# Scores by row groups only: the padded copies of Q leave a mixed attention and convolution kernel

## The chip, the cores and the metric

One core of one Trainium2 chip. The metric is the device time of one execution in microseconds; the kernel before is given as the median of three runs. The engines are named PE (matrix products), PEld (its weight loads), DVE, ACT, POOL and SP; SP, ACT and POOL also issue DMAs. "Granted clock" is the share of full speed that the throttle left the matrix engine.

## The reference

Two blocks read sequences of 2048 positions and 448 channels and are mixed by a gate per position. Block A is attention with 16 heads of 28 channels that share one key and one value head. Block B is a convolution over time, per channel, whose kernel K comes from 256 complex modes.

```python
g = sigmoid((x * gate_w).sum(-1))
# A
q = x @ wq ; k = x @ wk ; v = x @ wv              # q: 16 heads of 28; k, v: one head
p = softmax(q . k * 28 ** -0.5) ; a = concat(p @ v) @ wo
# B
K[d, l] = Re(sum_n C[d,n] * exp(dt[d] * A[d,n] * l) * dt[d] * B[d,n])     # l = 0 .. 2047
b = causal_conv(u, K) + u * Dskip
out = g * a + (1 - g) * b
```

## The kernel before

**Attention.** A score tile is one head of one group of four heads against 128 keys and 512 queries. There are 16 rounds (four query blocks by four head groups) of 64 tiles, 1024 tiles in all, taken in sets of three and two by turns; 410 sets. For each set PE writes the tiles into PSUM banks (`qk`), ACT takes the exponential of the whole set in one instruction (L1153), and two sets later PE multiplies four exponentials at a time with the values, each into 32 of 128 columns of the array (`pv`, L1163). Five PSUM banks hold scores, one holds the sums of a round, two are lent to everything else. ACT has nothing to do in the long run but these exponentials.

A score product has only 29 rows (28 channels and one for a bound of the maximum). The kernel has two forms. The row form (L1125) puts each head on its own 32 rows of the array, so that the tiles of one set run at the same time. The full form (L1133) uses all 128 rows with a copy of Q, `qM`, in which the rows of the other heads are zero; its tiles run one after the other. The first six sets are of row form, the next eight of full form, and from then on sets of three are of row form and sets of two of full form. `qproj` makes Q of a round on PE and DVE, and then four DMAs on POOL's queue copy it into `qM`, which POOL set to zero at the start.

**Convolution.** For each of 14 groups of 32 channels DVE builds tables of powers (`masters`, `tables`), PE multiplies them to K (`kgen`, L915) in two halves, each with its own PSUM bank and its own two evacuations by DVE (L926, L930), and POOL's queue writes K to memory. SP's queue then loads it back as Toeplitz blocks (`tload`, four channels each, 112 blocks) into one of four buffers in `T`, or, later on, into the used part of `U`. `conv` multiplies a block with `U`, the transposed input; four channels run at once, each on 32 columns of the array (L974). DVE scales, PE transposes back (L995), DVE adds to the output tile `O` (L1003).

**Order.** The order of each engine's instructions is fixed ahead by a list scheduler in `Prog.schedule`. It has a price for every operation, a constant for POOL's use of DVE's memory port (`PORT`), a slack for late consumers (`SLACK`), and a priority per operation; scores come first, convolution fills what is left. Engines take their instructions strictly in that order.

**End.** `norm` divides a round's sums by their last column. For the first 15 rounds the denominators go through memory on POOL's queue. For the last one PE gathers them (L1048), DVE takes 16 reciprocals per partition (L1052) and spreads them (L1054), PE transposes them back (L1059), and DVE multiplies 512 columns (L1063). `tail` makes the last projections (L1077) and adds them to `O` (L1021). All output goes out on SP's queue: the columns of the last two channel groups in one transfer of 64-byte pieces (`outz`), everything else ahead of it.

## Time and profile before

| | |
|---|---|
| median of 3 runs | 523.14 us (521.81 to 524.54) |
| the profiled execution, its own time | 521.35 us |
| its span, first to last instruction | 519.4 us |
| first exponential starts, last one ends | 27.7 us, 504.2 us |
| ACT, busy time of all / of the exponentials | 483.6 us / 465.8 us |
| PE, PEld, DVE, POOL, busy time | 431.1, 192.9, 447.5, 161.6 us |
| granted clock, mean of 27.7 to 112 us / of 112 to 504.2 us | 0.74 / 1.00 |
| DMA engines, mean busy share of the same two stretches | 0.71 / 0.94 |

An engine's busy time says how long it had an instruction in work; the busy time of PE includes the pipeline's latency, so PE can show as busy without being at its peak. What counts is which engine the others wait for: time in which ACT has no exponential is lost for good, and so is what lies ahead of the first exponential and behind the last.

### The profile page before, as it was taken

How to read it: one execution, taken by the hardware profiler on the slowest of the kernel's cores; microseconds unless marked ns; L12 is line 12 of the kernel's file. 1: busy time of each engine (PE TensorE's matmuls, PEld its weight loads, DVE VectorE, ACT ScalarE, POOL GpSimd, SP SyncE). 2: the span in 40 equal slices, each digit the busy share in tenths (PEclk: the TensorE clock that was granted, in tenths of full speed). 3: DMA queues.
4: the chain of work that ended last, by engine and by line, in shares of the span. 5: the costliest groups of instructions: out<-in, count | busy, mean ns of one | idle time of the engine just before them, and what ended most of it. 6: DMA issues, size and time to landing. Idle time of an engine off the chain costs nothing.

```text
span 519.4 us, 18307 instructions
## 1 busy us (share of the span) xinstructions
PE 431.1 (83%) x8123; PEld 192.9 (37%) x8234; DVE 447.5 (86%) x798; ACT 483.6 (93%) x431; POOL 161.6 (31%) x299
## 2 busy tenths in 40 slices
PE   5778967888878789988878889988888889798884
PEld 4522111324334334434333434433344344443342
DVE  3877899999999999999999979999999989952123
ACT  3699899999999999999999999999999999899980
POOL 5014321612413442424214242432414233315100
PEclk9858587979999999999999999999999999999998
DMA  8995395497991998899998899899996999999996
GB/s 263 259 236 157 28 79 139 120 364 251 288 365 54 321 350 256 271 342 347 316 367 296 279 373 276 285 336 350 329 330 212 304 370 353 346 282 305 376 365 172
DMA packets 121997, 144.31 MB, mean 278 GB/s; under 512 B 53860, under 2 KB 60564, under 8 KB 121920
## 3 DMA queue, kind: packets, MB, share of 16 engines
q1 hardware_dynamic: 112368, 133.06, 81.3%
q0 software_dynamic: 8896, 9.53, 6.8%
q8 instruction: 64, 1.05, 0.8%
q10 hardware_dynamic: 656, 0.57, 0.4%
q14 instruction: 13, 0.11, 0.1%
HBM read 128.76 MB, written 5.23 MB: 258 GB/s over the span
## 4 chain that ended last, share of the span: by engine, by line
ACT 40%; DVE 36%; PE 17%; DMA 3%; issue 2%; ACTq 0%; SPq 0%
ACT expT L1153 40%; DVE tab L868 6%; PE psS L1133 4%; DVE tab L880 3%; DVE tab L879 3%; DVE tab L878 3%; PE psB L1163 3%; PE psS L1125 3%; DVE tab L890 3%; DVE tab L877 3%; DMA T<-KP_scratch 2%; DVE tmp L886 2%; DVE msq L811 1%; DVE cst L984 1%; PE psX L915 1%
## 5 line engine op out<-in xcount | busy, mean ns | idle before, releaser
L1153 ACT ACTIVATE expT<-psS 128x1536 bf16<-128x1536 f32 (+1 forms) x410 | 465.8, 1349 | 8.1 <-PE psS L1125 5.3
L1133 PE MATMUL psS<-qM,kT 128*128 128x512 bf16 x308 | 106.6, 402 | 35.5 <-ACT expT L1153 21.7
L1125 PE MATMUL psS<-qT,kT 29*128 29x512 bf16 x609 | 84.0, 401 | 27.8 <-ACT expT L1153 23.4
L1163 PE MATMUL psB<-expT,vaug 128*32 128x512 bf16 x1024 | 105.4, 403 | 1.1 <-ACT expT L1153 0.6
L137 POOL DMA_DIRECT2D KP_scratch<-kstg x112 | 62.3, 563 | 121.3 <-DVE kstg L930 114.6
L868 DVE TENSOR_TENSOR tab<-tab,mbf 128x512 bf16<-128x512 bf16 (+3 forms) x56 | 64.5, 1152 | 0.0
L1163 PEld LDWEIGHTS psB<-expT,vaug 128*32 128x32 bf16 x1024 | 26.2, 93 | 83.2 <-issue 78.7
L137 POOL DMA_DIRECT2D qM<-qT x64 | 32.0, 507 | 67.9 <-DVE qT L786 42.9
L1125 PEld LDWEIGHTS psS<-qT,kT 29*128 29x128 bf16 x609 | 20.1, 91 | 72.6 <-ACT expT L1153 60.2
L1133 PEld LDWEIGHTS psS<-qM,kT 128*128 128x128 bf16 x415 | 26.0, 98 | 54.8 <-ACT expT L1153 40.2
L137 POOL DMA_DIRECT2D rdenB<-R_scratch x60 | 30.5, 514 | 38.5 <-DMA R_scratch<-denT 27.9
L880 DVE TENSOR_TENSOR tab<-tab 128x128 bf16<-128x128 bf16 (+4 forms) x70 | 41.8, 597 | 0.0
L879 DVE TENSOR_TENSOR tab<-tab 128x128 bf16<-128x128 bf16 (+4 forms) x70 | 41.8, 597 | 0.0
L974 PE MATMUL psS<-T,U 128*32 128x128 bf16 (+7 forms) x1600 | 39.0, 220 | 2.2 <-DMA T<-KP_scratch 1.3
L974 PEld LDWEIGHTS psS<-T,U 128*32 128x32 bf16 (+7 forms) x1600 | 27.1, 94 | 18.1 <-issue 12.2
L137 POOL DMA_DIRECT2D denT<-acc x15 | 10.9, 726 | 69.1 <-DVE acc L1030 45.0
L890 DVE TENSOR_TENSOR tab<-tab,tmp 128x4096 bf16<-128x4096 bf16 x14 | 32.1, 2290 | 0.1
L878 DVE TENSOR_TENSOR tab<-tab,mbf 128x4096 bf16<-128x4096 bf16 x14 | 31.9, 2280 | 0.1
L877 DVE TENSOR_TENSOR tab<-tab,mbf 128x4096 bf16<-128x4096 bf16 x14 | 32.0, 2283 | 0.0
L974 PE MATMUL psX<-T,U 128*32 128x128 bf16 (+7 forms) x1216 | 29.9, 223 | 1.0 <-issue 0.9
L974 PEld LDWEIGHTS psX<-T,U 128*32 128x32 bf16 (+7 forms) x1216 | 21.0, 95 | 14.7 <-issue 11.3
L915 PE MATMUL psX<-tab 128*32 128x64 bf16 x1024 | 24.8, 241 | 1.1 <-DVE qT L786 0.4
(153 smaller groups left out, 517.1 us busy)
## 6 DMA issues: line engine op xcount, KB each, us to landing
T<-KP_scratch SPq DMA_DIRECT2D x176, 512.0 KB, 8.7
U<-KP_scratch SPq DMA_DIRECT2D x48, 512.0 KB, 9.6
rdenB<-R_scratch POOLq DMA_DIRECT2D x60, 64.0 KB, 5.7
U<-cst SPq DMA_DIRECT2D x1, 3584.0 KB, 18.7
qM<-qT POOLq DMA_DIRECT2D x64, 32.0 KB, 5.1
tab<-in_A_x_dram SPq DMA_DIRECT2D x4, 448.0 KB, 6.2
O<-in_A_x_dram SPq DMA_DIRECT2D x16, 112.0 KB, 2.7
O<-cst SPq DMA_DIRECT2D x1, 1792.0 KB, 28.6
```

The lines of the kernel that those rows point to most:

```text
L137: return [e.dma_start(o, i, **kw) for o, i in pairs]
L868: vo(lambda e, dst=dst, src=src, mri=mri: e.tensor_tensor(dst, src, mri, ALU.mult), 4 * n, done + mk(lv), [kr, ki, tk])
L877: vo(lambda e, src=src, mi=mi, tv=tv: e.tensor_tensor(tv, src, mi, ALU.mult), 2 * n, done + mk(lv), [tk])
L878: vo(lambda e, dst=dst, src=src, mr=mr: e.tensor_tensor(dst, src, mr, ALU.mult), 2 * n, done + mk(lv), [kr, ki, ("gap", s)])
L879: vo(lambda e, dc=dc, tc=tc: e.tensor_tensor(dc[0], dc[0], tc[1], ALU.subtract), n, [tk, kr], [kr])
L880: vo(lambda e, dc=dc, tc=tc: e.tensor_tensor(dc[1], dc[1], tc[0], ALU.add), n, [tk, ki], [ki])
L890: vo(lambda e: e.tensor_tensor(tab.v(0, P, FM, [[4, 1024], [1, 4]]), tab.v(0, P, lo + 124, [[CG, 32], [-4, 32], [1, 4]]), rho.v(0, P, 0, [ ...
L974: r = e.matmul(ps.v(32 * j, 32 - 2 * n, 128 * k, [[1, 128]]), self.U.v(0, P, (4 * gi + j) * 32 + 2 * n, [[1, 32 - 2 * n]]), tbuf.v(0, P, t ...
L1125: r = e.matmul(self.psS.v(0, P, 512 * b, [[1, 512]]), kT.v(32 * h, DH + 1, 128 * kt, [[1, 128]]), qT.v(32 * h, DH + 1, 512 * (i % 2), [[1, ...
L1133: return e.matmul(self.psS.v(0, P, 512 * b, [[1, 512]]), kT.v(0, P, 128 * kt, [[1, 128]]), self.qM.v(0, P, (i % 2) * XQ + 512 * h, [[1, 51 ...
L1153: pg.op("act", lambda e: e.activation(expT.v(0, P, 512 * es[0], spread(es, n)), self.psS.v(0, P, 512 * bs[0], spread(bs, n)), AF.Exp, scal ...
L1163: r = e.matmul(self.psB.v(32 * h, 32, 0, [[1, 512]]), vaug.v(0, P, 32 * kt, [[1, 32]]), expT.v(0, P, 512 * ring[t], [[1, 512]]), start=(kt ...
```

## The change

All score sets take the row form. `qM`, its zeroing and its 64 DMAs go. The memory that they held becomes a fifth Toeplitz buffer. The rest comes with it:

- `kgen` writes both halves into one PSUM bank, and DVE evacuates them with two instructions instead of four; the eight DMAs follow together.
- `U` holds channels in pairs: POOL's eight copies move 4-byte units, the zero fill and the duplicating DMA have half as many pieces, and `conv` reads every second element. The filling of `U` is taken behind the preparation of the parameters, whose scratch moves from `mbf` to `O`.
- `masters` of the first block of channels writes its squares to the two buffers by turns.
- The last `norm` multiplies the sums with a matrix that puts each head's denominator on all of its 32 rows, in two halves of 256 columns; DVE takes reciprocals of all 256 columns and multiplies.
- The last four output tiles go out whole, two on ACT's queue and two on SP's, and `outz` covers only the first twelve.
- In the loads of the start, the weights of K and V come first and `log_dt` before `wq`.
- The scheduler's constants for POOL's port and for DVE's slack change, and one for DMA time. The order of all engines is planned anew with these.

```diff
-NTR = 4
+NTR = 5
...
-    PORT = 750.0
+    PORT = 0.7
...
-    SLACK = {"pe": 500.0, "dve": 1000.0}
+    SLACK = {"pe": 500.0, "dve": 500.0}
...
-                if e == "pool" and o.ns >= 900.0:
-                    free["dve"] = max(free["dve"], r) + self.PORT
+                if e == "pool" and o.ns >= 500.0:
+                    free["dve"] = max(free["dve"], r) + self.PORT * o.ns
...
-        self.qM = sb("qM", 2 * 4 * 512, BF)
...
-        for k in range(2):
-            pm(V(self.qM, k * XQ, XQ), 0.0, 1800, [("qM", k)], 1.5)
...
-            pg.dma([(self.qM.v(32 * h, 32, s * XQ + 512 * h, [[1, 512]]), self.qT.v(32 * h, 32, 512 * s, [[1, 512]]))
-                    for h in range(4)], (128, 1024), f"qm{s}", rd=[("q", s)], wr=[("qM", s)], pr=0, eng="pool", extra=4500)
...
-            if s < 6 or s >= 14 and len(ts) == 3:
-                rd = set()
-                ...
-                pg.op("pe", row, 220, rd=sorted(rd, key=str), wr=bk, pr=0, mode="q", ni=2 * len(ts))
-            else:
-                for t, b in zip(ts, bs):
-                    i, kt, h = dec(t)
-                    pg.op("pe", lambda e, t=t, b=b: full(e, t, b), 220, rd=[("qM", i % 2), ("kT", kt // 4)],
-                          wr=[("b", b)], pr=0, mode="f", ni=2)
+            pg.op("pe", row, 220, rd=sorted(rd, key=str), wr=bk, pr=0, mode="q", ni=2 * len(ts))
...
-                pg.op("pool", lambda e, k=k, j=j: e.tensor_copy(
-                    self.U.v(0, P, 8 * k + j, [[32, D], [1, 2]]),
-                    self.O.v(0, P, (8 * k + j) * D, [[1, D], [D, 2]])), 1080,
+                pg.op("pool", lambda e, k=k, j=j: e.tensor_copy(
+                    U2.v(0, P, 8 * k + j, [[32, D // 2], [1, 2]]),
+                    O2.v(0, P, (8 * k + j) * D // 2, [[1, D // 2], [D // 2, 2]])), 560,
...
-                                     self.U.v(0, P, (4 * gi + j) * 32 + 2 * n, [[1, 32 - 2 * n]]),
+                                     self.U.v(0, P, (2 * gi + j // 2) * 64 + 4 * n + j % 2, [[2, 32 - 2 * n]]),
...
+        pg.op("dve", lambda e: e.tensor_copy(ko.v(0, P, 0, [[64, 8], [1, 63]]), G.v(0, P, 0, [[64, 8], [1, 63]])),
+              el(504), rd=[X], wr=["kst"], pr=2, unlock=G)
...
+        for hf, b in enumerate((1, 6)):
+            ...
+            pg.op("pe", lambda e, bc=bc, hv=hv: e.matmul(bc, self.identf.v(0, P, 0, [[1, P]]), hv, start=True, stop=True,
+                                                         tile_position=(0, 0), skip_group_check=True),
+                  440, rd=[("acc", i % 2), "msq"], wr=[("b", b)], pr=0)
+            pg.op("dve", lambda e, bc=bc, rv=rv: e.reciprocal(rv, bc), el(256), rd=[("b", b)] + ["rd"] * hf, wr=[("rd", hf)] + ["rd"] * (1 - hf), pr=0)
+            pg.op("dve", lambda e, on=on, hv=hv, rv=rv: e.tensor_tensor(on, hv, rv, ALU.mult), el(256),
+                  rd=[("acc", i % 2), ("rd", hf)], wr=[("on", g + hf)], pr=0)
...
-            pg.dma([(dram(self.out, tl * P * D, [[D, P], [1, D0]]), self.O.v(0, P, D * tl, [[1, D0]]))],
-                   (128, 832), f"out{tl}", rd=[("O", 3)], pr=1)
...
+        pg.dma([(dram(self.out, D0, [[D, P], [P * D, 12], [1, 32]]), self.O.v(0, P, D0, [[D, 12], [1, 32]]))],
+               (1024, 64), "outz", rd=[("Oz", q) for q in range(3)], pr=1)
+            pg.dma([(dram(self.out, tl * P * D, [[D, P], [1, D]]), self.O.v(0, P, D * tl, [[1, D]]))],
+                   (128, 896), f"out{tl}", rd=[("O", 3 + tt), ("Oz", 3 + tt)], pr=1, eng=("act", "sp")[tt % 2])
```

## The prediction

> **What bounds the kernel now.** First the page, parts 1 and 5, then busy time by stretch.

> ```profile
> PE 431.1 (83%) x8123; PEld 192.9 (37%) x8234; DVE 447.5 (86%) x798; ACT 483.6 (93%) x431; POOL 161.6 (31%) x299
> ...
> L1153 ACT ACTIVATE expT<-psS 128x1536 bf16<-128x1536 f32 (+1 forms) x410 | 465.8, 1349 | 8.1 <-PE psS L1125 5.3
> L1133 PE MATMUL psS<-qM,kT 128*128 128x512 bf16 x308 | 106.6, 402 | 35.5 <-ACT expT L1153 21.7
> L1125 PE MATMUL psS<-qT,kT 29*128 29x512 bf16 x609 | 84.0, 401 | 27.8 <-ACT expT L1153 23.4
> ```

> ACT is the bound. From the first exponential (27.7) to the end of the last (504.2) pass 476.5 us, 465.8 of them exponentials and only 8.1 waiting, nearly always for PE's scores. The change leaves all 410 exponentials as they are. So it can gain at most those 8.1, something ahead of 27.7 and something of the 15.2 us behind 504.2; it can lose whatever makes PE late.

> Next, PE and the granted clock (columns: PE, PEld, DVE, ACT, POOL busy, clock, DMA share, GB/s):

> ```profile
> 50.60:54.00 3.40, 3.24 (x15) 0.59 (x15) 3.30 (x5) 3.40 (x3) 3.21 (x4) 0.50 0.00 0
> 54.00:57.40 3.40, 3.36 (x20) 0.56 (x16) 3.29 (x5) 3.35 (x4) 2.91 (x3) 0.50 0.00 0
> ...
> 60.80:64.20 3.40, 3.18 (x12) 0.62 (x12) 1.89 (x8) 1.55 (x3) 0.00 (x0) 0.50 0.77 59
> ...
> 101.80:105.20 3.40, 2.06 (x20) 0.52 (x20) 3.40 (x8) 3.40 (x4) 1.34 (x3) 1.00 0.89 298
> 105.20:108.60 3.40, 2.73 (x14) 0.48 (x12) 3.40 (x4) 3.40 (x4) 0.56 (x1) 0.50 1.06 399
> 108.60:112.00 3.40, 3.40 (x43) 1.16 (x43) 3.40 (x6) 2.47 (x3) 0.00 (x0) 0.50 1.06 392
> ...
> 27.70:112.00 84.30, 68.17 (x527) 19.72 (x536) 75.87 (x142) 80.04 (x71) 26.17 (x41) 0.74 0.71 150
> 112.00:504.20 392.20, 338.21 (x7266) 154.90 (x7366) 348.14 (x611) 388.75 (x344) 127.78 (x236) 1.00 0.94 310
> ```

> The clock is 1.00 or 0.50 and changes in steps of 3.41 us. Up to 112 us it is half in five stretches, although PE shows as 95% busy in some of them; from 112 on, when convolution fills PE, it never falls. At half clock ACT starves: 4.3 us are idle before 112, only 3.5 in the 392 us after.

> Last the exponentials' pace, the price of a reciprocal, and the end (start, duration, engine, line):

> ```profile
> 45.94 6.89 ACT expT L1153 x6
> ...
> 52.88 1.04 PE psS L1133 x2
> 53.92 0.55 PE psB L1163 x4
> 54.47 0.54 PE psS L1125 x3
> ```

> ```profile
> L655 DVE TENSOR_SCALAR gt<-gt x1: 158/158/158, 30.1 to 30.1; 128x16 f32<-128x16 f32 x1
> ...
> L1036 DVE RECIPROCAL denT<-denT x15: 240/244/270, 74.8 to 483.7; 128x16 f32<-128x16 f32 x15
> ```

> ```profile
> 504.67 0.69 DVE L1030 COPY acc<-psB 128x512 f32<-128x512 f32 x1 [1.08 <-PE psB L1163]
> ...
> 509.37 0.69 DVE L1063 TENSOR_TENSOR onT<-acc,psS 128x512 bf16<-128x512 f32 x1 [1.89 <-PE psS L1059]
> ...
> 514.01 0.42 DVE L1003 TENSOR_TENSOR O<-O,psS 128x256 bf16<-128x256 bf16 x1
> ```

> A pair of sets (five tiles) takes ACT 2.30 us. At half clock two full tiles take PE 1.04 us one after the other, three row tiles 0.54 together.

> **Score sets by row groups: what the clock follows.** From the records I placed every matrix product in time and counted its share of the array: rows of 128 times columns of 128, with 0.215 us for a pass of 512 columns (about what a second full tile adds at full clock). Summed over each step of 3.41 us, this use decides the next step's clock in all but one case: highest use followed by half clock 0.36 (50.6 to 57.4; 0.33 at 101.8), lowest followed by full clock 0.38 (173.5) and 0.39 (60.8, 405.6). The one exception is the step at 71.1. Time in which any product streams fits less well: the step at 47.2, with 0.47, is followed by half clock, the one at 405.6, with 0.43, by full.

> A pair of sets uses now 3 x 29/128 x 0.215 + 2 x 0.215 + 5 x 0.25 x 0.215 = 0.85 us of 2.30, or 0.37; the rest (convolution, K, projections) brings the steady stage (112 to 504) to 0.55. With row tiles the first two terms become 5 x 0.049: 0.51 us, or 0.22. The stage falls to about 0.41. Replacing the pairs in the records so, 35 of its 115 steps lie under 0.36, 53 under 0.38; now one or two do.

> Price of a step at half clock there: per pair, two sets 1.08, values 1.25 x 0.55 = 0.69, convolution 0.44 (896 groups of four at 0.1 over 205 pairs), K 0.18 (1792 at 21 ns, not stretched), projections 0.27, transposes 0.06: 2.72 us against 2.30. That is 0.53 us lost per step. The nearest row is 105.2 to 112, two half-clock steps with the first convolution: 0.93 lost, 0.47 each; before, without convolution, 0.34. I take 0.45. At that pace use is 0.93/2.72 = 0.34, so the clock tends to stay down; I take 45 steps, between 35 and 60. 45 x 0.45 = **+20 us**; ends 0 (the clock stays up) and 60 x 0.53 = +32.

> [...] The trace speaks against plain busy time, since three steps at 50.6 to 60.8 show PE over 90% busy and the clock stays at half. [...]

> Before 112 us, where the clock will now mostly be half, PE needs only 1.08 + 0.69 = 1.77 us per pair, so the stalls on full tiles go and those on projections (five passes of 0.43 in a burst) stay: of 4.3 us about 2 return. **-2** (-4 to +1).

> **qM's DMAs and zeroing.** 64 issues of 0.51 us leave POOL's queue, two memsets of 1.8 us its start; no engine but PE's full tiles waited for them: 0. PE's first product waits for x, not for POOL. 2 MB of 144 leave the DMA engines.

> **Start.** The exponential of the decays and two of the mq now follow the first score exponential (1.9 us of ACT moved behind it); the chain absolute maximum, Wb, Q is no longer behind a 1.05 us parameter product on DVE (L724 at 23.45); sine and K's last quarter come about 1 us earlier. First exponential near 26, with 1.9 us more to do: **0** (-1 to +1).

> **kgen, pairs in U, fifth buffer, planning.** DVE evacuates K with 14 x (0.17 + 0.68) instead of 28 x (0.17 + 0.41): 4 us less, beside exponentials; POOL's eight copies of 1.03 us halve, also beside. K's first half now waits for the second before it is written, some 2 us in a group's period of over 20. SP passes the second half of x only after DVE has read the scratch in `O`; the Toeplitz loads behind it still wait for K first. Reading U at every second element is bounded by L915's weight loads, which step by four: 117 ns against 93, beside products. Waits for blocks cost ACT 1.35 (at 454) and 0.80 (at 266); a fifth buffer should return about half. DVE is 99% busy from 100 to 300, so where the new order asks for tables earlier, PE waits in turn. **-1** (-3 to +3).

> **End.** Out go L1048 to L1063 with their waits: sums copied at 505.36, products' end 510.06. In come, per half, a product, a reciprocal of 256 columns and a multiply (0.41). Plain operations cost 0.141 + columns/960 us (158 ns for 16, 0.69 for 512). The reciprocal's 16 columns took 242 ns: if the extra 84 is fixed, 256 columns take 0.49; if it is per column, 0.14 + 256 x 0.0063 = 1.75. Both chained: first product ready at 506.4 behind six projections, then twice 1.75 + 0.35, 510.6. That is 0.6 later than now, but the projections of the first half are done by then (0.6 saved at L1021): 0. With 0.49 it would be -2.8. I take per column: nothing else would set this operation apart from a scalar one.

> [...]

> Now four row transfers and then `outz` are issued one after another, and the span ends 5.0 us after L1003. Two queues issue two or three each (0.45 each), land 1.8 to 3.1 later: 3.8. **-1.2**. Together -1.2 (-4 to +1.5).

> **Sum.** Profiled execution 521.35 (span 519.4): 521.35 + 20 - 2 + 0 - 1 - 1.2 = 537. The median of runs lies 1.8 above the profiled one: **539 us**. Its own range, by its ends: 526 to 553.

> **Rivals.** (1) The clock follows busy time, or its threshold lies a little lower, and stays up. For it: single steps at 0.38 did not close it. Against it: the fit above. Then 521.35 - 4.2 + 1.8 = 519, faster; it decides when fewer than 10 steps fall to half (10 x 0.45 pays for the gains). (2) Once down, the clock stays down, because PE at half clock delivers only 0.34: two thirds of the 170 pairs at 2.72 cost 113 x 0.42 = 48, so 567. Against it: bursts of K and convolution reach 0.6 and more. (3) The clock stays up, but PE waits for tables or blocks that the new order expects earlier: the 4 us are given back, 523, with DVE's 99% for it. That two row tiles might not run together is excluded by L1125's own sets.

> **Chances.** Forecast 0.45; rival 1 0.33 (0.25 of it faster, the rest within 0.5%); rival 2 0.14; rival 3 0.08, half within, half slower. A change of 0.5% (2.6 us) is about what can be told from none. Faster 0.25, same 0.12, slower 0.63. The range 515 to 560 leaves out only gains beyond 8 us (some 0.05) and most of rival 2 (0.12).

> **What would show it.** Granted clock of 112 to 504 near 0.8 with ACT idle some 20 us there, waiting for L1127's scores; in the steps at half clock, use at or under 0.36 in the step before. Right about the end: reciprocals of 1.7 us, last transfer landing under 4 us after the last addition to `O`. A clock of 1.00 after 112 proves the forecast wrong, and the time is then below 523.

## The result, and the profile after

The changed kernel takes **537.94 us** (median of 4 runs, 534.1 to 543.68); the kernel before, beside it, 523.84 (521.81 to 524.86). The ratio is 1.0254, 95% interval 1.0205 to 1.0302: slower. Ratios here and below leave out single executions that are over 1.5% longer than the fastest of the same kernel (here the one of 543.68). The profiled execution takes 534.4 us, its span is 532.7.

Parts 1, 2, 4 and 5 of its page:

```profile
PE 458.3 (86%) x8222; PEld 198.2 (37%) x8222; DVE 442.8 (83%) x771; ACT 486.8 (91%) x431; POOL 122.2 (23%) x233
...
PEclk9855557586697899999686999959796798995897
...
ACT 68%; PE 23%; DVE 1%; issue 1%; DVEq 0%
...
L1144 ACT ACTIVATE expT<-psS 128x1536 bf16<-128x1536 f32 (+1 forms) x410 | 469.4, 1291 | 20.3 <-PE psS L1127 19.7
L1127 PE MATMUL psS<-qT,kT 29*128 29x512 bf16 x1024 | 190.2, 458 | 49.4 <-ACT expT L1144 46.6
```

ACT still sets the time, but now waits 20.3 us instead of 8.1, nearly all of it for scores. PE has fewer passes to stream one after the other, but each is slower: a mean score product takes 458 ns where both forms took about 401. (PE's busy totals, 458.3 us and 431.1 before, cannot be compared: the trace before has 415 weight loads of full products and only 308 of the products.) The row of the granted clock says why they are slower; it is broken up to the end. The same by stretch (columns: PE, PEld, DVE, ACT, POOL busy, clock, DMA share, GB/s):

```profile
27.70:112.00 84.30, 71.58 (x615) 20.27 (x613) 74.93 (x145) 81.58 (x74) 17.52 (x29) 0.58 0.58 152
112.00:504.20 392.20, 349.66 (x7097) 155.28 (x7094) 339.35 (x574) 376.51 (x330) 101.26 (x184) 0.86 0.88 294
```

A mean of 0.86 over 392.2 us, from a clock that is 1.00 or 0.50, is 0.28 of 115 steps of 3.41 us at half clock: 32. Before, there was none. (In the clock records of both profiles every stretch from one change to the next is a whole number of steps of 3.413 us, those at half clock 1 to 18 steps long; only the last is cut by the end of the record.)

The account against the span before: the first exponential starts at 25.00 instead of 27.69 (-2.7); between the first and the last one ACT waits 12.2 us more, the exponentials themselves take 3.6 more (469.4 against 465.8), other work 0.6 more; from the end of the last one (517.93) to the end pass 14.8 us instead of 15.2 (-0.5). Sum 13.3 = 532.7 - 519.4.

The end, from the timeline (start, duration, engine, line):

```profile
520.35 1.76 DVE L1064 RECIPROCAL rdenB<-psS 128x256 f32<-128x256 f32 x1 [0.97 <-PE psS L1061]
522.14 0.42 DVE L1065 TENSOR_TENSOR onT<-acc,rdenB 128x256 bf16<-128x256 f32 x1
522.49 1.75 DVE L1064 RECIPROCAL rdenB<-psB 128x256 f32<-128x256 f32 x1
...
527.88 0.42 DVE L1016 TENSOR_TENSOR O<-O,psS 128x256 bf16<-128x256 bf16 x1 [0.22 <-PE psS L1008]
528.33 1.75 SPq L137 DMA_DIRECT2D out_dram<-O  x3
528.33 1.10 ACTq L137 DMA_DIRECT2D out_dram<-O  x2
```

The reciprocal is priced by its columns (1.76 and 1.75 us for 256, a median of 0.244 for 16 before and 0.245 after), the last addition is one of the convolution (L1016), and from it to the end of the span pass 4.4 us, 5.0 before.

### The profile page after: what moved, and what is told of

Read it like the earlier page. It is cut to its first block, busy times and chain, and to the rows that moved or that the text cites. A ratio compares the mean times of both kernels' runs of the same rounds, so it can differ in the third digit from the quotient of the medians.

```text
span 532.7 us, 18275 instructions
## 1 busy us (share of the span) xinstructions
PE 458.3 (86%) x8222; PEld 198.2 (37%) x8222; DVE 442.8 (83%) x771; ACT 486.8 (91%) x431; POOL 122.2 (23%) x233
## 3 DMA queue, kind: packets, MB, share of 16 engines
q8 instruction: 64, 1.05, 0.8%
## 4 chain that ended last, share of the span: by engine, by line
ACT 68%; PE 23%; DVE 1%; issue 1%; DVEq 0%
ACT expT L1144 67%; PE psS L1127 9%; PE psB L1154 5%; PE psS L987 3%; PE psX L987 2%; PE psS L927 1%; PE psX L782 1%; ACT mq L747 1%; PE psX L927 1%; DVE rdenB L1064 1%; PE psS L1079 0%; PE psS L1008 0%; DVE O L1034 0%; PE psS L782 0%; PE psX L1008 0%
## 5 line engine op out<-in xcount | busy, mean ns | idle before, releaser
L1144 ACT ACTIVATE expT<-psS 128x1536 bf16<-128x1536 f32 (+1 forms) x410 | 469.4, 1291 | 20.3 <-PE psS L1127 19.7
L1127 PE MATMUL psS<-qT,kT 29*128 29x512 bf16 x1024 | 190.2, 458 | 49.4 <-ACT expT L1144 46.6
L1154 PE MATMUL psB<-expT,vaug 128*32 128x512 bf16 x1024 | 121.5, 461 | 3.4 <-issue 2.9
L1127 PEld LDWEIGHTS psS<-qT,kT 29*128 29x128 bf16 x1024 | 40.6, 93 | 143.5 <-ACT expT L1144 113.7
L987 PE MATMUL psS<-T,U 128*18 128x128 bf16 (+7 forms) x1856 | 50.4, 240 | 0.2 <-DVE qT L794 0.2
L987 PEld LDWEIGHTS psS<-T,U 128*18 128x18 bf16 (+7 forms) x1856 | 35.5, 103 | 18.7 <-issue 13.4
L137 POOL DMA_DIRECT2D R_scratch<-denT x15 | 8.7, 578 | 111.5 <-DVE denT L1049 57.8
L898 DVE TENSOR_TENSOR tmp<-tmp,mq 128x64 bf16<-128x64 bf16 (+4 forms) x70 | 25.5, 364 | 0.1
L1043 DVE COPY acc<-psB 128x512 f32<-128x512 f32 x16 | 11.0, 689 | 16.0 <-PE psB L1154 13.7
```

What stands on the lines that cost most here:

```text
L137: return [e.dma_start(o, i, **kw) for o, i in pairs]
L987: r = e.matmul(ps.v(32 * j, 32 - 2 * n, 128 * k, [[1, 128]]), self.U.v(0, P, (2 * gi + j // 2) * 64 + 4 * n + j % 2, [[2, 32 - 2 * n]]), t ...
L1127: r = e.matmul(self.psS.v(0, P, 512 * b, [[1, 512]]), kT.v(32 * h, DH + 1, 128 * kt, [[1, 128]]), qT.v(32 * h, DH + 1, 512 * (i % 2), [[1, ...
L1144: pg.op("act", lambda e: e.activation(expT.v(0, P, 512 * es[0], spread(es, n)), self.psS.v(0, P, 512 * bs[0], spread(bs, n)), AF.Exp, scal ...
L1154: r = e.matmul(self.psB.v(32 * h, 32, 0, [[1, 512]]), vaug.v(0, P, 32 * kt, [[1, 32]]), expT.v(0, P, 512 * ring[t], [[1, 512]]), start=(kt ...
```

## The experiments

Times are medians; a ratio goes against runs of the kernel before on the same chip. The rows of the profile are 112 to 504.2 us by stretch, with the columns as above, unless a sentence says otherwise.

### The change without its row sets

```diff
-NTR = 5
+NTR = 4
...
+        self.qM = sb("qM", 2 * 4 * 512, BF)
...
+            if s < 6 or s >= 14 and len(ts) == 3:
...
+            else:
...
+                    pg.op("pe", lambda e, t=t, b=b: full(e, t, b), 220, rd=[("qM", i % 2), ("kT", kt // 4)],
...
```

> The changed kernel with one part undone: from the fifteenth set on, sets of two take the full form again (and the eight sets before, all), with the padded copies of Q and four Toeplitz buffers; everything else of the change stays. Theory (the clock falls because the array is used too little): granted clock 0.95 or more after 112 us, ACT idle under 5 us there, 517 to 521 us. Rival (the new order or the waits for tables and blocks cost the time, the clock only shows it): 530 us or more.

522.56 us, ratio 0.9984 (0.9949 to 1.002).

```profile
112.00:504.20 392.20, 352.57 (x7146) 152.15 (x7138) 332.19 (x553) 385.46 (x341) 126.05 (x232) 0.99 0.91 300
```

The clock is back and the loss gone: it lies in the row sets. The time is still above the theory's 517 to 521 us, and ACT idles 6.7 us from 112 to 504.2, not under 5. What is left of the change is worth nothing: the first exponential starts 3.0 us earlier (24.73), but ACT then waits 10.0 us in all instead of 8.1, the last exponential ends at 504.5 as before, and the last addition to `O` comes at 516.1 instead of 514.4.

### The row sets alone

```diff
-            if s < 6 or s >= 14 and len(ts) == 3:
+            if True:
```

> The kernel before with one part of the change alone: all sets of row form; the copies of Q are still made, and nobody reads them. Theory: granted clock 0.78 to 0.86 over the span, some 30 to 45 steps at half clock after 112 us, 534 to 545 us. Rival (the other parts cost the time): 521 to 526 us.

532.9 us, ratio 1.0178 (1.0118 to 1.0238). The profiled execution is the longest of the four (539.46):

```profile
112.00:504.20 392.20, 343.88 (x7085) 152.64 (x7086) 345.49 (x606) 376.98 (x331) 126.42 (x233) 0.88 0.90 296
```

In that execution the clock and ACT's busy time are near those of the changed kernel (0.86 and 376.51). Over the span the four have a clock of 0.82 to 0.86, the changed kernel 0.80 to 0.82, the kernel before 0.93 to 0.96. So the row sets alone bring most of the loss: by the ratios 9.3 us of 13. The time is a little under what was expected. The rest, worth nothing with full sets, seems to cost some 4 us with row sets, though the two intervals overlap.

### One more full product, ahead of the scores

Its result is overwritten by the first tile of the set; the planner does not count it.

```diff
             def row(e):
+                if len(ts) == 2 and not hasattr(e, "n"):
+                    i, kt, h = dec(ts[0])
+                    e.matmul(self.psS.v(0, P, 512 * bs[0], [[1, 512]]), kT.v(0, P, 128 * kt, [[1, 128]]),
+                             qT.v(0, P, 512 * (i % 2), [[1, 512]]),
+                             start=True, stop=True, tile_position=(0, 0), skip_group_check=True)
```

> The changed kernel with one more product ahead of each set of two, 128 rows by 128 columns by 512, into the first bank of the set, which the set then writes over. It adds 0.215 us of work and of use to each pair of sets (use 0.41 becomes 0.50). Theory, whether the clock follows the share of the array or the time in which products stream: clock 0.95 or more after 112 us, 516 to 521 us, although PE has more to do. Rival (PE is simply late): 540 us or more.

555.89 us, ratio 1.0637 (1.0587 to 1.0688): the clock did as expected, the time the opposite.

```profile
112.00:504.20 392.20, 363.45 (x7044) 158.84 (x7042) 341.69 (x572) 367.86 (x319) 100.05 (x182) 0.94 0.84 279
```

From 200 us on the clock is 0.95 to 0.97, but ACT idles 3.7 to 6.6 us in each 100, where it idled 0 to 2 before. The timeline of PE shows the reason (250.50 is the added product, then the two row tiles, then convolution):

```profile
250.50 0.39 PE L1127 MATMUL psS<-qT,kT 128*128 128x512 bf16 x1
...
250.82 0.39 PE L1132 MATMUL psS<-qT,kT 29*128 29x512 bf16 x2
...
251.14 0.35 PE L987 MATMUL psX<-T,U 128*32 128x128 bf16 x12
```

The row tiles follow 0.32 us after the full one and not 0.215, and the whole of it lies between an exponential and the scores that the next one waits for. A high clock is not enough where PE's own chain is too long.

### The same with a row product

```diff
-                    e.matmul(... kT.v(0, P, 128 * kt, [[1, 128]]), qT.v(0, P, 512 * (i % 2), [[1, 512]]) ... (0, 0))
+                    e.matmul(... kT.v(32 * h, DH + 1, 128 * kt, [[1, 128]]), qT.v(32 * h, DH + 1, 512 * (i % 2), [[1, 512]]) ... (32 * h, 0))
```

> The same with the added product on 29 rows only (the set's own first tile, made twice), so the same streaming time (0.215 us per pair, not beside the others) but a quarter of the share (0.049 us). If the clock follows the share of the array: 0.88 or less after 112 us, and each half-clock step costs more, 536 to 550 us. If it follows the time in which products stream: as with the full product, clock 0.95 or more, 516 to 522 us.

569.15 us (559.48 to 576.28), above the range; clock as expected:

```profile
112.00:504.20 392.20, 366.09 (x6580) 146.07 (x6573) 336.73 (x564) 347.77 (x300) 90.94 (x165) 0.82 0.80 263
```

As many passes of 512 columns as in the run above, in the same places, and the clock is 0.82 instead of 0.94. This profile is of the longest of the four; over the span their clocks are 0.78 to 0.82, those of the run above 0.87 to 0.88. What is streamed counts for more than that something is streamed.

### The clock by itself

The list of handfuls, written closer together than in the kernel:

```diff
+            phases = [[F, F, F], [F, F, FH], [F, F, FQ], [F, F], [F], [F, F], [F, F, FQ], [F, F, FH],
+                      [FZ, FZ, FZ], [FW, FW, FW], [R(0)] * 3, [R(0)] * 5, [R(0), R(1), R(2), R(3)] * 3,
+                      [R(0), R(1)] * 3, [C(0)] * 3, [C(0), C(1), C(2), C(3)] * 3]
...
+                for _ in range(24):
+                    pg.op("act", lambda e, k=k: e.activation(...), 1340, rd=["ps"], wr=[("e", k % 2)], pr=k)
+                    pg.op("pe", run(ph), 100, rd=keys + [("e", k % 2)], wr=["pb"], pr=k)
```

F is a product of 128 x 128 by 512 columns, FH and FQ by 256 and 128; FZ has 96 moving rows of zeros, FW weights of zero; R(g) has 29 rows of row group g and 128 columns, C(g) 128 rows and the 32 columns of column group g.

> Nothing of the reference is computed: the output is the input x, and the time says nothing. ACT runs exponentials of three banks without a break, some 1.36 us each; beside each PE makes a fixed handful of passes of 512 columns (0.215 us at full clock), 24 times the same, some 33 us or nine to ten steps of 3.41 us for each handful. If the clock follows the share of the array in use (rows times columns, threshold 0.36 to 0.38): three passes of 128 x 128 (0.47) full clock, two and a half (0.40) full, two and a quarter (0.36) on the edge, two (0.32) half, one half, and again on the way up; three passes with 96 moving rows of zeros, or with weights of zero, full; three or five 29-row passes one after the other (0.11, 0.18) half; four row groups at the same time, three times (0.43), full; two row groups, three times (0.21), half; three passes of 32 columns (0.12) half; four column groups, three times (0.47), full. If it follows the time in which anything streams: three and five 29-row passes, two row groups three times and 32 columns three times all stream 0.47 or more and have full clock. If zeros count for nothing, the passes with zeros fall to half. At the end PE runs long rows of passes without a wait: full and 29-row passes by turns take 0.32 us each if the change of form costs 0.1, 0.215 if not; 96 row passes alone fall to half clock by the share, stay at full by the time.

Busy time and clock by stretch, each stretch inside one handful; in order F3, F2.5, F2.25, F2, then (left out: one, two and 2.25 passes, 0.50 to 0.56) 2.5 on the way up, FZ3, FW3, R3, R5, four row groups three times, two row groups three times, C3, four column groups three times:

```profile
14.45:42.80 28.35, 18.22 (x62) 4.46 (x62) 0.00 (x0) 28.14 (x22) 0.00 (x0) 1.00 0.00 0
51.10:75.50 24.40, 14.10 (x54) 4.01 (x54) 0.00 (x0) 24.40 (x19) 0.00 (x0) 0.92 0.00 0
80.10:107.70 27.60, 21.40 (x62) 5.54 (x62) 0.00 (x0) 27.60 (x22) 0.00 (x0) 0.60 0.00 0
110.00:139.80 29.80, 22.38 (x44) 2.91 (x46) 0.00 (x0) 29.80 (x24) 0.00 (x0) 0.50 0.00 0
...
241.00:269.20 28.20, 16.97 (x62) 4.71 (x62) 0.00 (x0) 28.20 (x22) 0.00 (x0) 0.88 0.00 1
273.00:301.20 28.20, 17.04 (x62) 4.45 (x63) 0.00 (x0) 28.20 (x23) 0.00 (x0) 1.00 0.00 0
306.00:333.40 27.40, 16.37 (x60) 4.24 (x60) 0.00 (x0) 27.40 (x22) 0.00 (x0) 1.00 0.00 1
341.00:369.40 28.40, 27.49 (x58) 5.13 (x57) 0.00 (x0) 27.52 (x20) 0.00 (x0) 0.50 0.00 0
378.00:420.80 42.80, 42.80 (x102) 14.14 (x101) 0.00 (x0) 29.15 (x21) 0.00 (x0) 0.50 0.00 0
432.00:454.40 22.40, 15.20 (x200) 4.02 (x204) 0.00 (x0) 22.27 (x17) 0.00 (x0) 0.91 0.00 1
460.00:490.50 30.50, 28.45 (x124) 5.80 (x124) 0.00 (x0) 28.36 (x21) 0.00 (x0) 0.50 0.00 1
498.00:522.80 24.80, 14.90 (x55) 3.73 (x54) 0.00 (x0) 24.80 (x20) 0.00 (x0) 1.00 0.00 0
527.00:553.80 26.80, 16.57 (x244) 4.52 (x240) 0.00 (x0) 26.80 (x21) 0.00 (x0) 1.00 0.00 1
```

The edge lies where the prediction had it, between 2.25 passes in 1.36 us (0.36, a mean clock of 0.60 on the way down and 0.56 on the way up, so mostly half) and 2.5 (0.40, with 0.92 and 0.88 mostly full). The values do not matter here: with zeros, moving or as weights, the clock is 1.00. 29-row passes keep it at 0.50 even where PE streams without a break for 42.8 us. One row falls out: three passes of 32 columns use 0.12 of the array and have 1.00. So in these handfuls it is the rows fed, times the time, that counts; columns do not. Streaming time alone and the share of the array are both refuted.

At the end PE runs without a wait; in order 32 full passes, then 48 full and row passes by turns, then 29-row passes alone from 4 us after their start (the weight loads follow):

```profile
616.95:623.64 6.69, 6.69 (x33) 3.04 (x32) 0.00 (x0) 0.00 (x0) 0.00 (x0) 1.00 0.00 0
...
566.00:581.24 15.24, 14.98 (x48) 4.40 (x48) 0.00 (x0) 0.00 (x0) 0.00 (x0) 1.00 0.00 0
...
627.90:660.57 32.67, 32.67 (x79) 11.14 (x78) 0.00 (x0) 0.00 (x0) 0.00 (x0) 0.50 0.00 0
```

```profile
624.16 3.78 PEld L430 LDWEIGHTS psX<-X 29*128 29x128 bf16 x19 [0.42 <-issue]
...
628.57 0.15 PEld L430 LDWEIGHTS psX<-X 29*128 29x128 bf16 x1 [0.28 <-issue]
628.99 0.15 PEld L430 LDWEIGHTS psX<-X 29*128 29x128 bf16 x1 [0.28 <-issue]
```

Under 29-row passes that never stop, the loads follow each other by some 0.2 us for less than 4 us, and by 0.42 from then on. From first to last start a full pass takes 6.69/31 = 0.216 us, a full or row pass by turns 15.24/47 = 0.324: a change of form costs 0.108. Not only the row form pays it:

```profile
598.84:606.52 7.68, 7.68 (x78) 2.26 (x71) 0.00 (x0) 0.00 (x0) 0.00 (x0) 1.00 0.00 0
606.84:616.73 9.89, 9.57 (x71) 2.50 (x72) 0.00 (x0) 0.00 (x0) 0.00 (x0) 1.00 0.00 0
```

Here four passes of 32 columns, which run together, change 23 times with two row tiles (first line) and with two full passes (second). Less their streaming time, 4.9 and 7.5 us, that is 0.12 and 0.10 a change. So a score set of either form pays about the same next to the values or the convolution, and these changes do not set the two forms apart.

### Full form in every second set of two

```diff
-            if s < 6 or s >= 14 and len(ts) == 3:
+            if s < 6 or s >= 14 and (len(ts) == 3 or s % 4 == 1):
```

> The kernel before, with the full form only in every second set of two after the first fourteen sets. Theory (use of the array sets the clock, and the clock the time): use falls half the way, from 0.55 to 0.48 on the mean of the steady stage, fewer steps fall under the threshold than with row sets only, so a granted clock after 112 us of 0.92 to 0.98, ACT waiting 9 to 14 us, and 524 to 530 us. Rival (what costs is the change between row and full form, 0.1 us each, and the full sets' two passes one after the other; the clock is beside the point): half as many full sets cost half of it, 517 to 522 us.

525.1 us, ratio 1.0058 (1.003 to 1.0087), in the theory's range.

```profile
112.00:504.20 392.20, 325.45 (x7219) 152.30 (x7278) 345.67 (x607) 386.20 (x341) 127.49 (x235) 0.99 0.92 305
```

The rival fell: half as many full sets are not faster. But the clock is hardly touched after 112 us: 0.99, above the 0.92 to 0.98 that were expected, and ACT waits 9.5 us. The clock does not fall in line with the use, as a threshold would have it: by the means, 2 of 115 steps are at half clock here and 28 with row sets only. The times (3.0 us lost against 9.3) point the same way, but their intervals do not exclude that half the sets cost half.

### Useless work behind the values

```diff
+                if kt < 15:
+                    r = e.matmul(self.psB.v(0, P, 0, [[1, 512]]), self.zz.v(0, P, 0, [[1, P]]), vaug.v(0, P, 0, [[1, 512]]),
+                                 start=False, stop=False, tile_position=(0, 0), skip_group_check=True)
...
-            pg.op("pe", mm, 230, rd=["va"] + [("e", ring[t]) for t in ts], wr=[("b", 6)], pr=0.5, mode="c", ni=8)
+            pg.op("pe", mm, 450, rd=["va", "zz"] + [("e", ring[t]) for t in ts], wr=[("b", 6)], pr=0.5, mode="c", ni=8)
```

> The changed kernel, all sets of row form, with one more product of 128 rows and 128 columns by 512 behind each four products with the values but the last of a round: its weights are zero and it adds into the sums, so nothing of what is computed changes. It lies behind the values, not between an exponential and the scores that wait for it, and raises the use of the array by 0.215 in 1.84 us, 0.12, from 0.41 to 0.53 in the steady stage. Theory: the granted clock after 112 us goes back to 0.97 to 1.00, ACT's waits for scores from 19.7 to 5 to 9 us, and the time from 538 to 519 to 527, although PE has 52 us more to do at full clock. Rival 1 (PE is short of time, whatever its clock): 0.27 us more in a pair of sets, up to 0.5 at half clock, 550 to 570 us. Rival 2 (products with zero weights do not count for the clock): clock 0.75 to 0.82, 550 or more.

554.22 us, ratio 1.0632 (1.0595 to 1.0669): a miss on the time. By stretch and from the timeline (last exponentials, last addition):

```profile
112.00:504.20 392.20, 354.94 (x7069) 161.48 (x7157) 339.97 (x574) 382.73 (x336) 104.29 (x188) 0.98 0.83 277
```

```profile
493.81 22.47 ACT L1146 ACTIVATE expT<-psS 128x1536 bf16<-128x1536 f32 x20
...
546.83 0.42 DVE L1018 TENSOR_TENSOR O<-O,psX 128x256 bf16<-128x256 bf16 x1 [0.75 <-PE psX L1010]
```

The clock went back as expected, ACT waits 13.6 us instead of 19.7, and the exponentials end at 516.3, earlier than with the change. The loss lies behind them: the convolution ends 31 us after the last exponential. The planner had been told 450 ns for the values instead of 230. With the old price, in the wide run below, the convolution ends 1.5 us after it (518.2 and 516.7). So it was the experiment's own price that spoiled its time.

### The same work, wide and narrow, with the old price

```diff
+                if v >= 44 and kt < 15:
+                    r = e.matmul(self.psB.v(0, 32, 0, [[1, 512]]), self.zz.v(0, P, 0, [[1, 32]]), vaug.v(0, P, 0, [[1, 512]]),
+                                 start=False, stop=False, tile_position=(0, 0), skip_group_check=True)
...
# narrow: DH + 1 rows of zz and vaug in place of P
```

> The changed kernel with one product of 128 rows and 32 columns by 512 behind each four products with the values, from 112 us on (tile 176 and later, the last four of a round left out); its weights are zero and it adds into the sums of one head, so nothing that is computed changes. The planner has the old price for the values, so that the convolution is not planned behind the last round as with the first try. The run of the clock alone had full clock with three passes of 32 columns by 128 rows, and half with 29 rows: rows count, columns do not. Theory (the clock follows rows times time, the clock sets the time): mean clock after 112 us 0.97 to 1.00, ACT's waits for scores 5 to 10 us in place of 19.7, 521 to 527 us, although PE has 43 us more to do at full clock. Rival 1 (PE is short of time, not of clock): 545 to 560 us. Rival 2 (the share of the array counts, rows times columns, so 32 columns add only 0.03): clock 0.85 to 0.9, 540 to 555 us.

> The same as the run beside it, with 29 rows in place of 128 in each added product: as many products of as many columns in the same places, so the same time on PE at the same clock, but less than a quarter of the rows. Theory (rows times time): clock after 112 us 0.82 to 0.90, ACT waits 25 to 45 us for scores, 540 to 560 us. If the time that anything streams counts, it goes like the run beside it, 521 to 527 us at 0.97 or more. If the extra product does not disturb at all, whatever its rows, 536 to 540 us.

Wide: 529.65 us, ratio 1.0149 (1.0107 to 1.0191). Narrow: 594.04 us (580.32 to 601.79). First the wide one, then the narrow one:

```profile
112.00:504.20 392.20, 354.63 (x7336) 162.69 (x7345) 340.34 (x575) 377.46 (x330) 99.86 (x183) 0.97 0.89 298
...
L1160 PE MATMUL psB<-vaug,zz 128*32 128x512 bf16 x198 | 77.6, 392 | 0.1
L1160 PEld LDWEIGHTS psB<-vaug,zz 128*32 128x32 bf16 x198 | 19.1, 96 | 0.5 <-issue 0.4
```

```profile
112.00:504.20 392.20, 378.15 (x6159) 148.00 (x6162) 322.44 (x547) 327.51 (x280) 85.50 (x156) 0.77 0.77 254
...
L1160 PE MATMUL psB<-vaug,zz 29*32 29x512 bf16 x198 | 88.9, 449 | 0.0
L1160 PEld LDWEIGHTS psB<-vaug,zz 29*32 29x32 bf16 x198 | 17.9, 90 | 57.5 <-issue 57.5
```

The two kernels differ in the rows of one useless product, 128 or 29, and by at least 48 us (580.32, the fastest with 29 rows, against 531.96, the slowest with 128). With 128 rows the kernel is faster than the changed one without that work (ratios to before 1.0149 and 1.0254, intervals apart), although PE has some 43 us more to stream. With 29 rows the clock sinks to 0.77 in the profiled execution and to 0.76 to 0.80 over the spans of all four, against 0.89 to 0.91 with 128. That settles the clock, but not all of the difference in time: the narrow product also changes the form twice. Its weight loads come after 57.5 us of idle time in all, 0.29 for each of the 198, those of the wide one after 0.5. In the timeline of the wide run the added product starts 0.23 us after the values (514.38 and 514.61), and the convolution behind it starts at the same time. How much of the 48 us is the clock's was not separated. The wide one stayed 3 us above its range: ACT still waits 16.9 us for scores, some 7 of them from 400 to 500 us where the clock is 0.93, and part at full clock, since the product takes PE's time.

### Old planning constants

```diff
-    PORT = 0.7
+    PORT = 750.0
...
-    SLACK = {"pe": 500.0, "dve": 500.0}
+    SLACK = {"pe": 500.0, "dve": 1000.0}
```

With them go the rule that uses `PORT` and the constant for DMA time. What `PORT` prices shows in the profile before: beside POOL's eight copies (47.8 to 57.0 us) eight of DVE's instructions of L813, L815 and L831 take 0.95 to 1.58 us each, and 0.29 right before and after them; those of L811 take 0.41 to 0.42 as elsewhere. What the two engines share there was not shown. Once on the first experiment's kernel, once on the changed kernel alone:

> The changed kernel with the full form, qM and four Toeplitz buffers put back, as in the first run, and now also with the planner's constants of before (port, slack, DMA time): what is left of the change are the start, kgen in one bank, U in pairs, the end and the output queues. In the first run ACT waited 9.6 us for scores, 8.1 before, most of it in sets of row form in the middle, so that the 2.2 us saved before 112 us were given back. Theory (these waits come from the new planning, which asks for tables and blocks earlier than DVE and the queues deliver them): they fall to 7 or less, and the time to 516 to 520 us, ratio 0.990 to 0.996. Rival (they come from the other parts, and any plan has some): 520 to 525 us, ratio 0.996 to 1.004.

> The changed kernel with the planner's constants of before alone. All sets stay of row form, so the clock should fall as with the change: 0.82 to 0.90 after 112 us. Theory (the clock is the cause, the plan matters little): 532 to 541 us, the changed kernel having 538. If the new plan had a part in the loss (the kernel before with row sets only had 533, 5 us less than the changed one), 529 to 533 us. If the new plan alone made the loss, 520 to 525 us.

With full sets: 535.21 us, ratio 1.0222 (1.0179 to 1.0265), a miss to the other side. With row sets: 536.19, ratio 1.0249 (1.0203 to 1.0295), as the theory had it, with a clock of 0.89 after 112 us. From the timeline of the first (last addition of the convolution, last outputs):

```profile
510.26 0.60 ACT L1160 ACTIVATE expT<-psS 128x512 bf16<-128x512 f32 x1 [0.66 <-PE psS L1140]
...
530.95 0.42 DVE L1021 TENSOR_TENSOR O<-O,psX 128x256 bf16<-128x256 bf16 x1 [0.74 <-PE psX L1013]
531.40 1.10 ACTq L137 DMA_DIRECT2D out_dram<-O  x2
```

The exponentials end 6 us later than with the new constants, 5.6 of it before 112 us (ACT busy 78.3 of 86 us, with the new ones 83.9), and the convolution 15 us later. So the new constants do not cause the waits: with the old ones ACT waits 15.0 us instead of 10.0. What the row sets cost with the old plan can't be read from the two times, which are 1 us apart, since with full sets the end waits for the convolution. It shows in the exponentials: with row sets ACT waits 24.5 us and the last one ends at 522.0, with full sets at 510.9. That the rest of the change brings nothing net with its own plan stays as it was; which part gives the early start back was not settled.

## Why the prediction was right

Forecast 539, measured 537.94; 15.8 us more were added up for the profiled execution, 13.0 came. That the median came within 1.1 us is in part luck: the sum was 2.6 us too high for the profiled execution (537 against 534.4), and the median of the runs lies 3.5 above that one where 1.8 was taken. The range "by its ends", 526 to 553, is not what the ends of the terms add up to; that would be 511 to 562.

- **The clock (+20).** The right cause, shown three ways: full sets back, clock and time back; row sets alone, clock gone and most of the loss there; rows added by useless work, clock back and, by the ratios, over 5 us of the 13 returned. That 29 rows in the same places let the clock sink further bears it out. The size is too large: 45 steps were taken, 32 came up to 504 us (33 with the rest), under the low end of 35. The price was right: ACT's idle time after 112 us grew from 3.4 to 16.6, 0.40 a step, or 0.51 with the 3.6 us by which the exponentials grew; 0.45 was taken. The step that failed is that at half clock use stays at 0.34 and the clock tends to stay down. It opened again: with everything that PE does, rows make about 0.45 on the mean of the stage (an estimate from the products in its trace), above the 0.36 to 0.40 at which the clock by itself changed over.
- **What the clock follows.** The share of the array, rows times columns, was wrong in the columns. The kernel's narrow products nearly always run four side by side (in the timeline after, at 301 us, four products with the values take 0.40 us together and one single product 0.39), which makes the two alike, so the records before could not tell. By the author's count, an estimate from the products in the some 1800 steps of the profiles of all kernels here but the clock's own, rows times time (passes taken at their full-clock length) with one threshold of 0.365 misjudges the next clock in about one step of twenty, streaming time (0.42) in one of twelve, share of the array (0.325) in one of eleven. So the prediction's "all but one case" was a fit to few steps. By the same estimate rows fall in the steady stage from nearly 0.6 to about 0.45; half the row sets leave about 0.5. If streaming of any kind kept the clock up, the first rival would have come; the granted clock of 0.50 under 42.8 us of unbroken 29-row passes says that here it does not.
- **Before 112 us (-2).** ACT's idle time went from 4.3 us to 2.7: -1.6.
- **Start (0).** Too pessimistic: -2.7 at the first exponential, 0.6 more of other work behind it.
- **qM (0), and kgen, U, fifth buffer, planning (-1).** Not separated. Together with the start they are worth nothing with full sets (0.9984), so about 3 us must come back, by the traces as waits and a later convolution: the upper end, +3. That is the third rival in small. POOL's copies into `U` went from a median of 1.03 us to 0.66, not to half.
- **End (-1.2).** -0.5. The reciprocals took 1.75 and 1.76 us, the value per column; the products end 6.8 us after the last exponential instead of 5.9 (+0.9, 0.6 foreseen), the last addition comes 10.4 after it instead of 10.3, and the tail is 4.4 and not 3.8.
- **The rivals.** The clock fell, against the first; it opened again, against the second; and with full sets the loss was gone, against the third.

## What to carry to other kernels

Packing products into row groups saves the time of a pass (at half clock three row tiles took 0.54 us together, two full ones 1.04), but takes rows from the measure that the clock followed here. Before such a change, add up rows/128 times streaming time over 3.41 us and see that it stays, in every step and not in the mean, clear of the stretch from 0.36 to 0.40, in which the clock by itself went from mostly half (0.56 and 0.60) to mostly full (0.88 and 0.92). Where PE has spare time, the wide form with rows of zeros can be the cheaper one: with it in the sets of two the changed kernel took 522.56 us, without it 537.94. And when an experiment adds work, look first at where it lies on the chain and what the planner does with its price.
